# Keys with queries, and v, in two tiles; their loads issued in the middle of a step of the recurrence

## The chip, the cores and the metric

The kernel runs on one core of a Trainium2 chip. A core has TensorE (PE in the rows; its weight loads are PEld), VectorE (DVE), ScalarE (ACT), GpSimd (POOL) and SyncE (SP), which issues most transfers. The metric is the time of one execution on the device in microseconds, as the median of several.

## The reference, cut to what matters

Three stages follow each other. The change lies in the first.

```python
# q, k, v, f_logit: [B=4, H=8, S=768, D=48], f32
f = 1.0 / (1.0 + np.exp(-f_logit))
for t in range(S):                       # gated linear attention
    state = f[:, :, t, :, None] * state + np.einsum('bhd,bhe->bhde', k[:, :, t], v[:, :, t])
    y[:, :, t] = np.einsum('bhd,bhde->bhe', q[:, :, t], state)
x = y as [3072, 384]
# soft mixture of 8 experts: softmax of x @ phi over tokens, two weight products an expert, softmax back
# then gate * val @ w_out, with gate = sigmoid(x @ w_gate), val = x @ w_val
```

## The kernel before, in words

The recurrence is cut into 24 steps: 6 chunks of T = 128 positions (u) times 4 batches (b), step i = 4u + b. A step handles all 8 heads of one batch and one chunk. The order on each engine is the order in which the code is written; a pool only adds the waits that its tiles need. Work is written ahead, so that step i also prepares steps i + 1 to i + 5.

What stands in step i, in this order:

- POOL: `prep_k(i+1)` (line 326, two instructions: the keys times decays e, in place in the tile of keys), `z_stage(i+1)` (lines 335 and 337: the state times a decay, into sb), `prep_c(i+3)` (line 298: a clamp on the gate logits f).
- ACT: `conv_a(i+1)` in steps 1, 4, 7, 10, 13 and 16 alone (line 425: reads a raw piece of a gate weight), `prep_a(i+3)` (lines 302 and 303, on f), `prep_e(i+2)` (lines 316 and 317: decays e and rx from the sums s), copies of x and of transposed keys (lines 162 and 153), `y_out(i)` (line 403: empties y).
- PE: `a_stage(i)` (line 349, queries with keys), `y_inter(i)` (line 385, the products with the state sb), `prep_s(i+2)` (line 310, sums s of f), `kv(i)` (line 367), transposes (lines 159 and 152), in every fourth step `l_stage` (line 169) and in the one after it the products of lines 202 to 221, and at the end `y_intra(i)` (line 397, the masked products with v).
- DVE: `m_stage(i)` (line 356), `prep_q(i+1)` (line 330, queries times rx), z and the conversion of raw weights.
- SP: `load_f(i+5)`, in six steps a raw piece (`load_raw`, 512 KB), one load of expert weights (768 KB), and last `load_kq(i+3)`.

Keys, queries and v of one step lie in one tile `kqv` of 128 x 1408 numbers (704 KB), filled by one transfer; there are three such tiles, taken in turn (i % 3). So `load_kq(i+3)` overwrites what step i reads, and SP holds it until the last reader is done: `y_intra(i)`, which reads v. SP issues in order, and a transfer that waits holds up those behind it.

y and s each have one PSUM tile: `y_inter(i+1)` waits until `y_out(i)` has emptied y, and `prep_s(i+2)` until line 317 has read s.

Of the kernel before, what the change touches and what calls it, by code (L numbers as in the profile page):

```python
# [17 lines left out]
B, H, S, D = 4, 8, 768, 48  # L18
DM = H * D
TH = 64  # L20
HP = H // 2
T = 128
NU = S // T
# [6 lines left out]
NG = DFF // GW  # L30
QF = NF // NG
CONV_AT = 2, 5, 8, 11, 14, 17
KQ = 2 * HP * T
LOAD_FROM, LOAD_TO = 1, NSTEP - 1
WARM = 10, 1, 0, 0, 3, 1
BIG = 3.4e38
# [3 lines left out]
HUGE = float(np.uint32((1150 << 20) | 0xFFFFF).view(np.float32))  # L40


def body(ctx, tc, fn, fd, kqv, phi, w1, w2, wg, wv, wo, out_t):
    nc = tc.nc
    V, A, PE, PO, SP = nc.vector, nc.scalar, nc.tensor, nc.gpsimd, nc.sync

# [82 lines left out]
    def attention_in(att, aps, slow):  # L129
        def at(shape, tag, dt=F32):  # L130
            return att.tile(shape, dt, tag=tag, name=tag)
# [17 lines left out]
        def kt_stage(k, kts):  # L149
            ps = pt([128, HP, 112], "m", 2, "ktp")  # L150
            for h in range(HP):
                PE.transpose(ps[:, h], k[0:112, h], ident[0:112, 0:112])
            A.copy(kts, ps)
# [60 lines left out]
        def d2b(u):  # L214
            d2b_mm(u)
            d2b_add(u)
# [22 lines left out]
        def fast_steps():  # L239

            kq, vts, ft = [None] * 3, [None] * 3, [None] * 3

            def inputs(i):
                t = at([128, KQ + DM], f"kqv{i}")
                kq[i] = t[:, 0:KQ].rearrange("p (k h t) -> p k h t", k=2, t=T)
                vts[i] = t[:, KQ:].rearrange("p (j c) -> p j c", j=2)
                kqvs[i] = t

            kqvs = [None] * 3
            rrs = [at([128, 2, 2, T], f"r{j}") for j in range(2)]  # L250
            mask = at([128, 2, T], "mask")
            inputs(2)
# [38 lines left out]

            def load_kq(i):
                u, b = divmod(i, B)
                SP.dma_start(kqvs[i % 3], kqv[u, b])


            def prep_c(i):
                PO.tensor_scalar(ft[i % 3], ft[i % 3], FMIN, None, op0=ALU.max)  # L298
# [147 lines left out]
            def once(fn, i, *a):  # L446
                if 0 <= i < NSTEP:
                    fn(i, *a)
# [5 lines left out]
            load_f(1)  # L454
            load_f(2)
            load_kq(1)
            prep_c(0)
            make_tri()
            prep_c(1)
# [26 lines left out]
            for i in range(NSTEP):  # L486
                u, b = divmod(i, B)
                more = u < NU - 1
                cv = conv(i)

                if i:
                    once(prep_k, i + 1, PO)
                    once(z_stage, i + 1, PO)
                once(prep_c, i + 3)
                conv_a(i + 1)

                a_stage(i)
                for j in range(2):
                    m_stage(j)
                if i >= B:  # L500
                    y_inter(i)
                if i == 0:
                    kt_stage(kq[0][:, 0], kts)

                once(prep_a, i + 3)
                once(prep_s, i + 2)
                once(load_f, i + 5)
                load_raw(CONV_AT.index(i + 2) if i and i + 2 in CONV_AT else NP if i == CONV_AT[-1] + 1 else -1)
                load_weights(i, 0)
                once(prep_e, i + 2)  # L510
                if i:
                    once(prep_q, i + 1, V)

                cv[0]()
                cv[1]()
                if more:
                    kv(i)
                    z_add(i)

                if i:  # L520
                    x_stage(i - 1)
                if i + 1 < NSTEP - B:
                    kt_stage(kq[(i + 1) % 3][:, 0], kts)
                if i >= 4 and b == 0:
                    l_stage(u - 1)
                    d1(u - 1)
                if i >= 4 and b == 1:
                    d2(u - 1)
                    d1b(u - 1)
                cv[2]()  # L530
                cv[3]()
                y_intra(i)
                y_out(i)
                if i >= 4 and b == 1:
                    d2b(u - 1)
                if i >= 4 and b == 0:
                    d1e(u - 1)
                once(load_kq, i + 3)
                if i == NSTEP - 3:
                    constants()  # L540

        def slow_steps():
            wt = [at([128, HP, T], f"w{i}") for i in range(2)]
            kk = at([128, HP, T], "k")
            vts = [at([128, 2, HP * D], f"v{i}") for i in range(2)]
            qq = at([128, HP, 2, T], "q")
            kts = at([128, HP, 112], "kt")
            zps = [pt([128, 2, HP, D], f"z{i}") for i in range(2)]
            aps_ = [pt([128, 2, 2, T], f"a{i}") for i in range(2)]

            def slow_step(i):
                u, b = divmod(i, B)
                w = wt[1][0:112]
                for j in range(2):
                    d = slice(64 * j, 64 * j + D)
                    SP.dma_start(wt[1][d], fd[u, b, j])
                    SP.dma_start(kk[d], kqv[u, b, d, 0:HP * T])
                    SP.dma_start(qq[d, :, j], kqv[u, b, d, HP * T:KQ].rearrange("d (h t) -> d h t", t=T))
                SP.dma_start(vts[i % 2], kqv[u, b, :, KQ:].rearrange("t (j c) -> t j c", j=2))
                A.activation(w, w, AF.Exp, scale=-1.0)  # L560
                V.tensor_scalar(w, w, 1.0, None, op0=ALU.add)
                V.reciprocal(w, w)
                kt_stage(kk, kts)
                vv, s, q = vts[i % 2], sb[i % 2], qq
                vo, vm = [t.rearrange("p j (h e) -> p h j e", e=D) for t in (vv, vts[(i + 1) % 2])]
                z = zps[b % 2][:, b // 2]
                with tc.For_i(0, T, 1) as t:
                    V.tensor_tensor(
                        z[0:112], z[0:112], w[:, :, bass.ds(t, 1)].to_broadcast([112, HP, D]), op=ALU.mult
                    )  # L570
                    for h in range(HP):
                        V.tensor_tensor(
                            vm[:, h], vo[:, h], (ident, wt[0].rearrange("p h t -> p (h t)"))[h % 2][:, None, bass.ds(t, 1)].to_broadcast([128, 2, D]),
                            op=ALU.mult,
                        )
                    for h in range(HP):
                        for j in range(2):
                            PE.matmul(
                                z[64 * j:64 * j + D, h], kts[:, h, 64 * j:64 * j + D],
                                vts[(i + 1) % 2][:, j, h * D:h * D + D],  # L580
                                start=False, stop=True, skip_group_check=True,
                            )
                    V.tensor_copy(s[0:112], z[0:112])
                    for h in range(HP):
                        PE.matmul(
                            aps_[h // 2][0:D, h % 2, :, bass.ds(t, 1)], s[0:112, h], q[0:112, h, :, bass.ds(t, 1)],
                            start=True, stop=True, skip_group_check=True,
                        )
                for h in range(2):
                    for g in range(2):  # L590
                        A.copy(yts[i % 4][64 * h:64 * h + D, 2 * g:2 * g + 2], aps_[g][0:D, h])

            V.memset(wt[1][32:64], 30.0)
            V.memset(kk[32:64], 0.0)
            for t in zps + aps_:
                V.memset(t, 0.0)
            load_phi(SP)
            constants()
            for t in [qq] + yts:
                PO.memset(t, 0.0)  # L600
            for p in range(E * 2):
                load_w1(*divmod(p, 2))
            for e in range(3):
                load_w2(e, slice(0, 8))
            load_wo(0, 11)
            r = wt[0].rearrange("p h t -> p (h t)")
            V.tensor_copy(r[:, 0:TH], ident[:, TH:T])
            V.tensor_copy(r[:, TH:T], ident[:, 0:TH])
            for i in range(NSTEP):
                u = i // B  # L610
                slow_step(i)
                if i == NSTEP - 1:
                    break
                x_stage(i)
                if i % B == B - 1:
                    l_stage(u)
                    d1(u)
                    d1e(u)
                    d2(u)
                    d1b(u)  # L620
                    d2b(u)
# [5 lines left out]
        mb, u = mrun[(NU - 1) % 2], NU - 1  # L627
# [414 lines left out]
```

## Time and profile before

| | us |
|---|---|
| median of 3 executions | 403.28 (403.27 to 405.97) |
| the profiled execution | 405.25 |
| its span, first to last instruction | 403.5 |
| PE busy | 354.2 (88%) |
| DVE busy | 224.5 |
| ACT busy | 212.2 |
| POOL busy | 193.3 |

1.75 us of the profiled execution lie outside its span. The 24 steps of the recurrence end at about 165 us of the span; the experts and the gated product fill the rest. The mean granted clock of PE is 0.977 of full speed. The busy shares are means over stages with different limits; what the change touches is read from the stretch of the 24 steps.

### The profile page before, as it was taken

The page shows a single profiled execution, that of the slowest core. Times are in us where ns is not written, and L with a number is a line of the kernel's source. Part 1 is how long each engine was busy: PE and PEld are TensorE (multiplying, and loading weights), DVE is VectorE, ACT ScalarE, POOL GpSimd, SP SyncE. Part 2 cuts the span into 40 slices and gives each one's busy share as a digit, 9 for nine tenths or more (in the row PEclk, how much of TensorE's full clock was granted, in tenths as well). Part 3 has the DMA queues.
Part 4 walks back from the last instruction along what each step waited for, and adds up shares of the span by engine and source line. Part 5 has one row for each costly group of instructions (what it writes and reads, how often), then busy time and mean ns, then how long its engine had stood idle before and what let it go on. Part 6 is the DMA issues. An engine that isn't in the chain of part 4 may idle for free.

```text
span 403.5 us, 9261 instructions
## 1 busy us (share of the span) xinstructions
PE 354.2 (88%) x3790; PEld 275.0 (68%) x3790; DVE 224.5 (56%) x419; ACT 212.2 (53%) x437; POOL 193.3 (48%) x210
## 2 busy tenths in 40 slices
PE   2877996969877958999788999999999999999993
PEld 2766775757666846734456887688888787888882
DVE  2763654562635534468628776536777667444442
ACT  4556572746466534323456766566555465544440
POOL 5265537355365433002116666465565556655550
PEclk9998998998999998999989999999999999999999
DMA  6667896795878895599500421040000000222222
GB/s 227 233 211 280 272 325 234 261 345 206 282 277 313 305 410 226 218 373 411 251 0 0 158 80 79 0 156 2 0 0 2 0 2 1 78 80 78 78 81 87
DMA packets 15588, 66.81 MB, mean 166 GB/s; under 512 B 1728, under 2 KB 5168, under 8 KB 14000
## 3 DMA queue, kind: packets, MB, share of 16 engines
q1 hardware_dynamic: 15408, 66.07, 44.5%
q8 instruction: 32, 0.52, 0.5%
q14 instruction: 20, 0.16, 0.1%
q10 hardware_dynamic: 128, 0.06, 0.0%
HBM read 61.40 MB, written 4.72 MB: 164 GB/s over the span
## 4 chain that ended last, share of the span: by engine, by line


## 5 line engine op out<-in xcount | busy, mean ns | idle before, releaser
L890 POOL TENSOR_TENSOR hl<-sg,hh 128x512 fp32r<-128x512 f32 x72 | 99.7, 1385 | 84.7 <-ACT hh L888 75.4
L886 DVE TENSOR_TENSOR sg<-sg,gvp 128x512 f32<-128x512 f32 x72 | 49.5, 687 | 68.6 <-ACT sg L885 68.2
L918 PE MATMUL oup<-hh,wo 128*128 128x512 f32 x216 | 84.8, 392 | 1.5 <-ACT acc L900 1.3
L919 PE MATMUL oup<-hh,wo 128*128 128x512 f32 x216 | 84.1, 389 | 0.0
L888 ACT CAST hh<-sg 128x512 fp32r<-128x512 f32 x72 | 44.8, 622 | 55.8 <-DVE sg L886 55.8
L326 POOL TENSOR_TENSOR kqv<-kqv,e 112x256 f32<-112x256 f32 x44 | 33.9, 792 | 71.0 <-DMA kqv<-kqv 46.8
L885 ACT ACTIVATE sg<-gvp 128x512 f32<-128x512 f32 x72 | 42.9, 596 | 17.3 <-PE gvp L880 16.9
L918 PEld LDWEIGHTS oup<-hh,wo 128*128 128x128 f32 x216 | 40.5, 188 | 12.0 <-ACT acc L900 1.7
L356 DVE TENSOR_TENSOR r<-a,mask 128x512 f32<-128x512 f32 x48 | 30.9, 685 | 29.7 <-PE a L349 29.6
L919 PEld LDWEIGHTS oup<-hh,wo 128*128 128x128 f32 x216 | 40.5, 188 | 8.2
L925 PE MATMUL oup<-hl,wo 128*128 128x512 f32 x162 | 45.6, 390 | 0.0
L880 PE MATMUL gvp<-cs,gs 128*128 128x512 f32 x144 | 44.7, 392 | 0.4 <-DVE sg L886 0.2
L310 PE MATMUL s<-tri,f 128*48 128x128 f32 x384 | 30.3, 308 | 9.6 <-ACT f L303 6.2
L302 ACT ACTIVATE f<-f 128x384 f32<-128x384 f32 x24 | 12.5, 522 | 45.3 <-POOL f L298 45.3
L925 PEld LDWEIGHTS oup<-hl,wo 128*128 128x128 f32 x162 | 30.3, 188 | 6.5 <-POOL hl L890 0.2
L310 PEld LDWEIGHTS s<-tri,f 128*48 128x48 f32 x384 | 23.2, 138 | 14.5 <-POOL tri L272 6.0
L298 POOL TENSOR_SCALAR f<-f 128x384 f32<-128x384 f32 x24 | 29.7, 1238 | 4.1 <-DMA f<-fn 4.0
L880 PEld LDWEIGHTS gvp<-cs,gs 128*128 128x128 f32 x144 | 26.9, 188 | 6.9 <-ACT gs L871 0.7
L706 POOL TENSOR_TENSOR wo<-wf,wo 128x384 fp32r<-128x384 f32 x12 | 12.2, 1016 | 38.7 <-PE hp L748 25.9
L385 PE MATMUL y<-kqv,sb 48*48 48x128 f32 x320 | 13.9, 289 | 16.3 <-ACT yt L403 10.0
L397 PE MATMUL y<-r,kqv 128*48 128x128 f32 x384 | 26.8, 283 | 0.4 <-DVE r L356 0.4
L397 PEld LDWEIGHTS y<-r,kqv 128*48 128x48 f32 x384 | 20.4, 126 | 4.8 <-issue 1.8
(153 smaller groups left out, 563.6 us busy)
## 6 DMA issues: line engine op xcount, KB each, us to landing
kqv<-kqv SPq DMA_DIRECT2D x24, 704.0 KB, 5.9
w<-w SPq DMA_DIRECT2D x22, 768.0 KB, 6.3
f<-fn SPq DMA_DIRECT2D x24, 192.0 KB, 3.5
rawo<-wo SPq DMA_DIRECT2D x3, 1536.0 KB, 7.5
w2p<-w SPq DMA_DIRECT2D x3, 1536.0 KB, 10.6
out_t<-os SPq DMA_DIRECT2D x17, 256.0 KB, 2.1
w<-w SPq DMA_DIRECT2D x2, 1536.0 KB, 8.1
rawg<-wg SPq DMA_DIRECT2D x2, 1536.0 KB, 7.5
```

The lines of the kernel that those rows point to most:

```text
L310: PE.matmul(sps[64 * j:64 * j + D, h], w[:, h, j], tri, start=True, stop=True, skip_group_check=True,)
L326: eng.tensor_tensor(k[:, h], k[:, h], e[:, h, :, ::1 - 2 * h], op=ALU.mult)
L356: V.tensor_tensor(rrs[j].rearrange("p g h t -> p g (h t)"), aps_[:, j].rearrange("p g h t -> p g (h t)"), mask.rearrange("p h t -> p (h t) ...
L397: PE.matmul(yps[64 * h:64 * h + D, j, g], vv[:, j, c:c + D], rrs[j][:, g, h], start=(i < B and g == 0), stop=True, skip_group_check=True,)
L880: PE.matmul(p, gs[n, k][:, o:o + 128], cs[:, u].rearrange("p b t -> p (b t)"), start=True, stop=True)
L885: A.activation(sg, ps[0], AF.Sigmoid)
L886: V.tensor_tensor(sg, sg, ps[1], op=ALU.mult)
L888: A.copy(h, sg)
L890: PO.tensor_tensor(l, sg, h.bitcast(F32), op=ALU.subtract)
L918: PE.matmul(ops[u][c], wh[q][:, fq, cc[c]], h, start=(fq == 0), stop=False)
L919: PE.matmul(ops[u][c], wl[q][:, fq, cc[c]], h, start=False, stop=False)
L925: PE.matmul(ops[u][c], wh[q][:, fq, cc[c]], l, start=False, stop=False)
```

## The change

Keys and queries lie in a tile `kq` of 128 x 1024 (512 KB), v in a tile of 128 x 384 (192 KB). Each has three buffers. Their loads stand right behind `y_inter(i)` in the code, ahead of `load_f(i+5)`: `load_kq(i+3)` and `load_v(i+2)`. At the start, v of steps 0 and 1 is loaded behind the keys of step 1. On the host the array `kqv` is given as two arrays. No instruction of another engine is added, dropped or moved. (Line numbers behind the edits differ by some lines.)

```diff
-def body(ctx, tc, fn, fd, kqv, phi, w1, w2, wg, wv, wo, out_t):
+def body(ctx, tc, fn, fd, kqd, v, phi, w1, w2, wg, wv, wo, out_t):
...
             def inputs(i):
-                t = at([128, KQ + DM], f"kqv{i}")
-                kq[i] = t[:, 0:KQ].rearrange("p (k h t) -> p k h t", k=2, t=T)
-                vts[i] = t[:, KQ:].rearrange("p (j c) -> p j c", j=2)
-                kqvs[i] = t
-
-            kqvs = [None] * 3
+                kq[i] = at([128, 2, HP, T], f"kq{i}")
+                vts[i] = at([128, 2, HP * D], f"v{i}")
+
...
             def load_kq(i):
                 u, b = divmod(i, B)
-                SP.dma_start(kqvs[i % 3], kqv[u, b])
+                SP.dma_start(kq[i % 3].rearrange("p k h t -> p (k h t)"), kqd[u, b].rearrange("p k c -> p (k c)"))
+
+            def load_v(i):
+                u, b = divmod(i, B)
+                SP.dma_start(vts[i % 3], v[b, u * T:(u + 1) * T].rearrange("t (j c) -> t j c", j=2))
...
             load_f(1)
             load_f(2)
             load_kq(1)
+            load_v(0)
+            load_v(1)
             prep_c(0)
...
                     y_inter(i)
                 if i == 0:
                     kt_stage(kq[0][:, 0], kts)
+                once(load_kq, i + 3)
+                once(load_v, i + 2)
 
                 once(prep_a, i + 3)
                 once(prep_s, i + 2)
...
                     d1e(u - 1)
-                once(load_kq, i + 3)
                 if i == NSTEP - 3:
                     constants()
```

On SP, steps 5 to 7 before (step 6 has a raw piece). A row is a transfer with its tile, its source and its shape; kqv is the joint tile, f the gate logits, w expert weights, raw a piece of the gate weights:

```order
L290 DMA f_130<-fn 128x384
L96 DMA w_1_523<-w 128x1536
L294 DMA kqv_116<-kqv 128x1408
L290 DMA f_129<-fn 128x384
L418 DMA raw<-wg 128x1024
L96 DMA w_2_720<-w 128x1536
L294 DMA kqv_126<-kqv 128x1408
L290 DMA f_131<-fn 128x384
L96 DMA w_2_720<-w 128x1536
L294 DMA kqv_121<-kqv 128x1408
```

and the same steps now (kq of steps 8, 9 and 10, v of steps 7, 8 and 9):

```order
L290 DMA kq_116<-kq 128x1024
L294 DMA v_123<-v 128x384
L286 DMA f_133<-fn 128x384
L95 DMA w_1_534<-w 128x1536
L290 DMA kq_128<-kq 128x1024
L294 DMA v_117<-v 128x384
L286 DMA f_132<-fn 128x384
L418 DMA raw<-wg 128x1024
L95 DMA w_2_733<-w 128x1536
L290 DMA kq_122<-kq 128x1024
L294 DMA v_129<-v 128x384
L286 DMA f_134<-fn 128x384
```

The load of step i + 3's keys has moved from behind the step's weights to ahead of its f, and what it waits for is `y_inter(i)`; v has a row of its own, one step nearer to its use, and waits for `y_intra(i-1)`, which is past by then.

The start of SP before:

```order
L290 DMA f_129<-fn 128x384
L294 DMA kqv_121<-kqv 128x1408
L290 DMA f_131<-fn 128x384
L290 DMA f_130<-fn 128x384
L418 DMA raw<-wg 128x1024
L294 DMA kqv_116<-kqv 128x1408
L290 DMA f_129<-fn 128x384
L294 DMA kqv_126<-kqv 128x1408
```

and now:

```order
L286 DMA f_132<-fn 128x384
L290 DMA kq_122<-kq 128x1024
L294 DMA v_129<-v 128x384
L294 DMA v_123<-v 128x384
L286 DMA f_134<-fn 128x384
L286 DMA f_133<-fn 128x384
L418 DMA raw<-wg 128x1024
L290 DMA kq_116<-kq 128x1024
L290 DMA kq_128<-kq 128x1024
L294 DMA v_117<-v 128x384
L286 DMA f_132<-fn 128x384
```

The keys of step 2 keep their place behind the raw piece; those of step 3 now follow them at once, ahead of the f of step 5.

## Rows read from the trace of the kernel before

**Rows 1.** Windows from one a_stage to another, then two shorter ones; columns in the first line.

```profile
core 0: us, PE busy (x) PEld busy (x) DVE busy (x) ACT busy (x) POOL busy (x), PEclk, DMA share, GB/s
16.50:43.05 26.55, 20.35 (x402) 17.15 (x401) 13.11 (x23) 14.94 (x34) 16.15 (x23) 0.94 0.75 260
43.05:70.96 27.91, 22.68 (x461) 18.70 (x459) 15.81 (x29) 15.25 (x37) 14.20 (x21) 0.94 0.77 267
70.96:98.15 27.19, 22.77 (x460) 18.70 (x459) 13.51 (x26) 15.60 (x38) 14.06 (x20) 0.94 0.76 266
98.15:124.57 26.42, 21.16 (x461) 17.45 (x459) 12.75 (x25) 15.74 (x39) 11.34 (x18) 1.00 0.86 300
124.57:147.39 22.82, 19.91 (x437) 16.19 (x435) 12.34 (x24) 11.54 (x29) 11.29 (x16) 1.00 0.88 329
147.39:164.70 17.31, 12.82 (x235) 9.57 (x236) 7.10 (x15) 7.58 (x23) 6.13 (x12) 0.90 0.56 221
164.70:403.50 238.80, 225.67 (x1232) 169.88 (x1229) 142.32 (x261) 122.43 (x221) 112.56 (x85) 0.99 0.24 94
67.40:70.70 3.30, 3.30 (x46) 2.80 (x48) 1.30 (x5) 0.34 (x1) 2.13 (x4) 0.50 0.06 18
138.00:148.00 10.00, 8.21 (x193) 6.81 (x193) 4.01 (x9) 2.93 (x7) 4.43 (x7) 1.00 1.01 417
```

**Rows 2.** Waits from 20 to 164 us: us in total, times, longest.

```profile
POOL kqv L326 <- DMA kqv<-kqv: 46.8, 10, 7.1
ACT f L302 <- POOL f L298: 41.1, 15, 6.2
...
PE y L385 <- ACT yt L403: 10.0, 5, 4.1
...
PE l L169 <- ACT x L162: 5.7, 4, 3.7
```

**Rows 3.** Timeline of steps 10 to 12: start, us, instruction, idle before it and its releaser.

```profile
79.64 0.60 ACT L316 ACTIVATE e<-s 112x512 f32<-112x512 f32 x1 [0.26 <-PE s L310]
...
82.66 0.65 PE L385 MATMUL y<-kqv,sb 48*48 48x128 f32 x16
...
83.38 2.18 POOL L326 TENSOR_TENSOR kqv<-kqv,e 112x256 f32<-112x256 f32 x2 [5.10 <-DMA kqv<-kqv]
...
84.79 0.33 SPq L290 DMA_DIRECT2D f<-fn  x1
...
86.33 1.60 POOL L298 TENSOR_SCALAR f<-f 128x384 f32<-128x384 f32 x1
...
87.22 0.33 SPq L294 DMA_DIRECT2D kqv<-kqv  x1
87.96 0.52 ACT L302 ACTIVATE f<-f 128x384 f32<-128x384 f32 x1 [5.45 <-POOL f L298]
...
90.73 0.63 ACT L403 COPY yt<-y 112x512 f32<-112x512 f32 x1
...
91.50 1.11 PE L385 MATMUL y<-kqv,sb 48*48 48x128 f32 x16 [3.54 <-POOL gg L335]
```

**Rows 4.** Transfers by kind: count, KB each, median us from issue to landing.

```profile
kqv<-kqv SPq DMA_DIRECT2D x24, 704.0 KB, 5.9
...
f<-fn SPq DMA_DIRECT2D x24, 192.0 KB, 3.5
...
raw<-wg SPq DMA_DIRECT2D x3, 512.0 KB, 4.2
```

**Rows 5.** Timeline of ACT in step 7.

```profile
56.35 0.69 ACT L425 ACTIVATE wgv<-raw 128x512 f32<-128x512 f32 x1 [1.75 <-DMA raw<-wg]
```

**Rows 6.** Timeline of PE, the a_stage of steps 7 and 8.

```profile
53.90 0.90 PE L349 MATMUL a<-kqv 48*64 48x128 f32 x32
...
58.63 0.90 PE L349 MATMUL a<-kqv 48*64 48x128 f32 x32
```

**Rows 7.** Timeline of POOL, the prep_k of steps 2 and 3.

```profile
24.13 1.33 POOL L326 TENSOR_TENSOR kqv<-kqv,e 112x256 f32<-112x256 f32 x2 [1.68 <-ACT e L316]
...
29.21 1.33 POOL L326 TENSOR_TENSOR kqv<-kqv,e 112x256 f32<-112x256 f32 x2 [1.68 <-ACT e L316]
```

More of the change, by code (lines that the diff above doesn't have):

```diff
@@ L32 @@
 CONV_AT = 2, 5, 8, 11, 14, 17
-KQ = 2 * HP * T
 LOAD_FROM, LOAD_TO = 1, NSTEP - 1
@@ L556, in slow_step @@
                     SP.dma_start(wt[1][d], fd[u, b, j])
-                    SP.dma_start(kk[d], kqv[u, b, d, 0:HP * T])
-                    SP.dma_start(qq[d, :, j], kqv[u, b, d, HP * T:KQ].rearrange("d (h t) -> d h t", t=T))
-                SP.dma_start(vts[i % 2], kqv[u, b, :, KQ:].rearrange("t (j c) -> t j c", j=2))
+                    SP.dma_start(kk[d], kqd[u, b, d, 0])
+                    SP.dma_start(qq[d, :, j], kqd[u, b, d, 1].rearrange("d (h t) -> d h t", t=T))
+                SP.dma_start(vts[i % 2], v[b, u * T:(u + 1) * T].rearrange("t (j c) -> t j c", j=2))
                 A.activation(w, w, AF.Exp, scale=-1.0)
@@ L1009 @@
         "f": np.ascontiguousarray(heads_t(f_logit)),
-        "kqv": np.concatenate([
-            np.pad(
-                np.stack([kr.reshape(NU, B, 2, D, HP * T), heads_t(q)], axis=4),
-                ((0, 0), (0, 0), (0, 0), (0, 64 - D), (0, 0), (0, 0)),
-            ).reshape(NU, B, 128, KQ),
-            vr.reshape(B, NU, T, DM).transpose(1, 0, 2, 3),
-        ], axis=3),
+        "kq": np.pad(
+            np.stack([kr.reshape(NU, B, 2, D, HP * T), heads_t(q)], axis=4),
+            ((0, 0), (0, 0), (0, 0), (0, 64 - D), (0, 0), (0, 0)),
+        ).reshape(NU, B, 128, 2, HP * T),
+        "v": np.ascontiguousarray(vr.reshape(B, S, DM)),
         "phi": np.pad(
```

## The prediction, made before the changed kernel ran

> **What bounds the kernel now.** I read the windows first, cut at an a_stage every fourth step, so that five stretches B to F follow the first one, A [rows 1]. Behind 164.70 us PE works 225.67 of 238.80 us: that part is set by its own products, and the change has no instruction in it. Of the 24 steps, A loses 6.2 us of PE time (26.55 - 20.35), and B to F lose 5.23, 4.42, 5.26, 2.91 and 4.49, together 22.3. PE also works part of the time at half clock: in 67.40 to 70.70 it was granted 0.50 of full speed, which is the lower of its two levels (1.2 GHz), after it had idled in front of the product of line 169. The cost is the stretch times one minus the granted share: 27.91 x 0.06, 27.19 x 0.06 and 17.31 x 0.10, so 1.7, 1.6 and 1.7 in B, C and F, together 5.0. So 27.3 us are lost in B to F, and no engine is full there: POOL, DVE and ACT each work about half of the time.
>
> What ends these waits is seen in the table of waits [rows 2]. PE waits for y to be emptied (10.0 us) and for copies of x (5.7). ACT, which empties y and copies x, waits 41.1 us for POOL's clamp on f. And POOL waits 46.8 us in ten waits for the transfer of kqv, up to 7.1 us. The timeline shows how one of these becomes PE's wait [rows 3]. Step 11's prep_k starts at 83.38, 5.10 us after POOL's last work, released by the transfer. The decay e that it also needs was done at 79.64 + 0.60 = 80.24, so 3.1 us of it are the transfer's alone. The clamp stands behind prep_k on POOL and runs at 86.33, ACT starts on f at 87.96 after 5.45 us idle, and everything behind that on ACT is late: y of step 11 is emptied at 90.73 to 91.36. POOL's next state comes in the same moment, and y_inter of step 12 starts at 91.50, 3.54 us late. That is one chain, transfer, POOL, ACT, PE, and it closes on itself, since SP issues the next kqv only when PE is through with y_intra.
>
> **The change, part by part.** The load of the keys is held by y_inter in place of y_intra. In step 11 y_inter ends at 82.66 + 0.65 = 83.31 and the load went out at 87.22: 3.9 us earlier now, more in steps where PE waits between the two. It also carries 512 KB in place of 704 and stands ahead of f and the step's weights on SP. A transfer of 704 KB landed after 5.9 us, one of 512 KB (raw) after 4.2, in the median [rows 4]; so the keys should be there some 1.7 us sooner still, 5.6 us in all. The transfer's own share of the wait was 3.1 us in step 11. I therefore take these waits as gone, and what is late next on POOL is e, which comes from ACT.
>
> What comes back must be taken off the 27.3 us. First, without a late transfer POOL and ACT feed each other in a round of their own: prep_k, clamp, ACT's work on f and e, next prep_k. In steps 2 and 3, where POOL waited for e and for no transfer, it took 29.21 - 24.13 = 5.08 us [rows 7]. A short step of PE takes 58.63 - 53.90 = 4.73 [rows 6]. Two of four steps are that short (the others have line 169, or lines 202 to 221, on top), so each of B to E keeps 2 x 0.35, together 2.8 us. Below that it can't go unless POOL works faster; if the long steps give the lag back it is nothing.
>
> Second, the raw pieces. ACT reads one in five steps, ahead of its work on f, and in step 7 it stood 1.75 us for it [rows 5]. Its load is held by prep_s through the f in front of it, so it goes out no earlier than now, and what stood ahead of it as kqv of the step before, issued at that step's end, is now kq and v of this step, issued just ahead. It can land earlier, if the steadier flow keeps the queue short, or later by up to the difference of the medians of 704 KB and 192 KB, 5.9 - 3.5 = 2.4 us. The transfer that it most resembles is itself, so I take 1.75 us as the wait in each of B to E, 7.0 in all; the bounds are 0 and 4 x (1.75 + 2.4) = 16.6. Third, the copies of x that line 169 waits for are ACT's, and ACT stays busier in that step than in others: a quarter of the 5.7 us, 1.4, stays (bounds 0 and 5.7).
>
> Edits at nothing: the 24 further issues of v cost SP 0.33 us each (the time of the issue in rows 3), 7.9 us in all, but SP mostly waits; what they push back are f, used two steps later, weights, used after the recurrence, and raw, counted above. v lands a step before kv reads it; if it did not, PE would stand in line 367. In stretch A, the keys of step 2 keep their place behind f and raw; the stretch is paced by the round of 5.08 us [rows 7], which nothing shortens, so I take 0; the bounds are 0 and the 1.7 us by which a smaller transfer landed sooner.
>
> Sum: 27.3 - 2.8 - 7.0 - 1.4 = 16.1 us less. The end moves with the recurrence, since PE is full behind it. The profiled execution of 405.25 would become 389.2; it stood 1.97 above the median, 403.28, which becomes 387.2.
>
> **Rivals.**
>
> *The transfer queues are full.* The 16 engines are busy 0.77, 0.76, 0.86 and 0.88 of B to E [rows 1], so 21.5 + 20.7 + 22.7 + 20.1 = 85.0 of 104.3 us. The forecast takes about 10 us out of these four (F gives the rest), which leaves 94: 90% busy. In D, 22.7 us of transfers would stand in some 24. Then keys would wait behind the weights of the step before, and POOL would wait for transfers as now, less often. For it speaks that the rate in B and C is 267 GB/s at 0.77, so no more than 350 at full; against it, that 138 to 148 moved 417 GB/s, in long rows of weights. Half of the waits gone would be 8 us less: 395. The Trainium skill (DMA: Bandwidth & Descriptors, Specifications) gives about 358 GB/s as the limit of HBM for a core; by it the 30.1 MB of B to E (27.91 x 267 + 27.19 x 266 + 26.42 x 300 + 22.82 x 329) would take an estimated 84 us, the same floor as the busy sum, and the end could not come below about 383. The 417 GB/s of that window speak against it as a limit.
>
> *Raw becomes the bound: slower.* Kq and v go out ahead of raw in the same burst. ACT reads raw ahead of f, so a late piece holds up decays, copies and the emptying of y in five steps. Without the raw term the sum is 23.1 us; raw would have to hold ACT 23.1 / 5 = 4.6 us a time for nothing to be left. At 6 us, which is 704 KB in the queue ahead of it (5.9 us), with nothing else ahead, the five cost 30 and the kernel takes 403.3 + 30 - 23.1 = 410. Against it: in step 11 the f, which stands ahead of raw, went out at 84.79, 1.5 us after the end of y_inter at 83.31 [rows 3], so the first 1.5 us of those 5.9 are past when raw goes out.
>
> *Hidden behind the recurrence, or not earlier at all.* The load is held by y_inter, and y_inter is what comes late; or the expert weights, which keep the pace of the steps, are not there when the recurrence ends sooner. F has its transfers busy for 0.56 of 17.31 us, so 7.6 us of room stand against the second, and step 11 against the first. If only the half-clock cost and F's idle were won back, 5.0 + 4.5 less the terms that stay there, it would be about 4 us less than now: 399.
>
> **How the numbers follow.** One per cent is 4.0 us, about what a measurement of this kernel can tell from no change. Forecast: 0.70. Full queues: 0.18. Raw as the bound: 0.06. Little won: 0.06. The range's lower end takes raw and the round at half their terms: 27.3 - 1.4 - 3.5 - 1.4 = 21.0, and 1.7 of stretch A, 22.7 less: 380. The upper end is full queues with raw late as well, a third of the forecast's gain, 5 less: 398. Faster by over 1%: 0.70, 0.15 of the full queues, 0.02 of the last, 0.87. Within 1%: 0.03 + 0.04 and a little of raw, 0.08. Slower: 0.05.
>
> **What would show it.** Right: in the table of waits, POOL for the transfer of kq falls from 46.8 us to under 10, POOL for e takes its place, and ACT's wait for the clamp halves. The stretches B to E last 23 to 25 us each (E 20 to 21) and have one half-clock piece at most; the transfer share is about 0.9. Raw's step: ACT's waits for raw in line 425 add up to about 7 us; if they reach 20, the second rival is right. Full queues: transfer share over 0.95, kq landing later than 6 us in the median. The forecast is wrong if y_inter still waits over 8 us in all while POOL no longer waits for kq: then ACT's own order would have been the bound.

## The result and the profile after

| | before | changed |
|---|---|---|
| median of 4 executions each, us | 404.58 (403.27 to 405.97) | 393.5 (391.84 to 394.98) |
| profiled execution, us | 405.25 | 393.43 |
| its span, us | 403.5 | 391.7 |

The ratio is 0.9725, 95% interval 0.9665 to 0.9784: faster by 2.75%, 11 us. The forecast was 387.2 with a range of 380 to 398. That forecast started from a median of 403.28, to which a fourth execution has been added since. The sign and the range hold; of the 16.1 us forecast, 11 to 12 came.

The windows of the changed kernel, cut at the same a_stage rows as [rows 1], A to F and the rest:

```profile
core 0: us, PE busy (x) PEld busy (x) DVE busy (x) ACT busy (x) POOL busy (x), PEclk, DMA share, GB/s
16.81:41.32 24.51, 19.92 (x402) 17.26 (x401) 13.06 (x23) 14.87 (x34) 16.53 (x23) 0.93 0.82 289
41.32:68.95 27.63, 22.60 (x461) 18.54 (x459) 15.13 (x29) 15.23 (x37) 14.47 (x20) 0.94 0.81 274
68.95:92.77 23.82, 21.10 (x461) 17.60 (x459) 13.38 (x26) 15.33 (x38) 12.96 (x20) 0.99 0.84 286
92.77:120.72 27.95, 22.70 (x461) 18.36 (x459) 12.88 (x25) 15.97 (x39) 13.19 (x21) 0.94 0.85 302
120.72:140.92 20.20, 19.86 (x437) 16.19 (x435) 12.93 (x24) 14.08 (x35) 10.53 (x16) 1.00 0.79 289
140.92:152.99 12.07, 11.40 (x235) 8.43 (x236) 7.70 (x15) 5.14 (x16) 4.36 (x8) 1.00 0.98 400
152.99:391.70 238.71, 225.57 (x1232) 169.91 (x1230) 142.39 (x261) 122.43 (x221) 112.61 (x85) 0.99 0.24 94
```

Beside [rows 1] the first column of each row, its length, changes like this. The last line splits the forecast by stretch: PE's loss and its half-clock cost, less what the prediction left of the round, of raw and of the copies.

| stretch | A | B | C | D | E | F | rest |
|---|---|---|---|---|---|---|---|
| before, us | 26.55 | 27.91 | 27.19 | 26.42 | 22.82 | 17.31 | 238.80 |
| after, us | 24.51 | 27.63 | 23.82 | 27.95 | 20.20 | 12.07 | 238.71 |
| difference | -2.0 | -0.3 | -3.4 | +1.5 | -2.6 | -5.2 | -0.1 |
| forecast | 0 | -4.1 | -3.2 | -2.5 | -0.1 | -6.2 | 0 |

With 0.3 us at the start these add up to the 11.8 us between the spans. The total looks like a forecast that is a third too large; by stretch it is something else. C came as forecast, F 1.0 short of it, A and E gave 2.0 and 2.5 more, and B and D together gave nothing where 6.6 us were expected. The gain is missing in two places, and the waits point at why.

The waits of the changed kernel from 20 to 153 us (us in total, times, longest):

```profile
POOL kq L326 <- ACT e L316: 49.1, 17, 5.1
...
ACT f L302 <- POOL f L298: 19.7, 12, 2.7
...
PE l L168 <- ACT x L161: 6.4, 4, 3.0
POOL kq L326 <- DMA kq<-kq: 6.4, 2, 5.2
ACT wgv L425 <- DMA raw<-wv: 6.3, 3, 3.0
...
PE y L385 <- ACT yt L403: 5.8, 3, 2.9
...
ACT wgv L425 <- DMA raw<-wg: 3.7, 1, 3.7
```

Against [rows 2] the first chain is gone: POOL's wait for keys fell from 46.8 us in ten waits to 6.4 in two, and ACT's wait for the clamp from 41.1 to 19.7. POOL now waits 49.1 us for the decays e, which come from ACT. Line 425, ACT's reading of a raw piece, waits 10.0 us in four waits (6.3 + 3.7). Before, its waits were 1.75 [rows 5], 0.54 and 1.50, so 3.8.

The timeline of steps 6 to 8 in B shows what hangs on one of them (start, us, instruction, idle before it and its releaser):

```profile
50.57 0.43 SPq L418 DMA_DIRECT2D raw<-wg  x1
...
52.58 1.16 POOL L298 TENSOR_SCALAR f<-f 128x384 f32<-128x384 f32 x1
...
56.61 0.67 ACT L425 ACTIVATE wgv<-raw 128x512 f32<-128x512 f32 x1 [3.74 <-DMA raw<-wg]
...
57.19 0.51 ACT L302 ACTIVATE f<-f 128x384 f32<-128x384 f32 x1
...
58.16 0.58 ACT L316 ACTIVATE e<-s 112x512 f32<-112x512 f32 x1
...
58.82 2.15 POOL L326 TENSOR_TENSOR kq<-kq,e 112x256 f32<-112x256 f32 x2 [5.08 <-ACT e L316]
...
59.95 0.63 ACT L403 COPY yt<-y 112x512 f32<-112x512 f32 x1
...
60.72 0.66 PE L385 MATMUL y<-kq,sb 48*48 48x128 f32 x16 [2.92 <-ACT yt L403]
...
65.47 0.82 PE L168 MATMUL l<-yt,phs 112*32 112x128 f32 x16 [1.81 <-ACT x L161]
```

It is the chain of [rows 3] with another head. The clamp on f was done at 53.74, so ACT could have gone on with f by then. It stands in line 425 until 56.61 for a piece that went out at 50.57, and f, e, prep_k, the emptying of y and y_inter follow late one after the other. PE loses 2.92 us here, 1.81 more in line 168, and has a half-clock piece behind it: in 65.40 to 68.90 it was granted 0.56 of full speed, and B as a whole 0.94, as before. By stretch, line 425 waits 3.74 us in B, 2.12 in C and 1.24 + 2.99 in D. B and D, with the most, are the two stretches without a gain; C gained in spite of its wait.

Did the piece come later, or did ACT come sooner? The same piece before, its issue and that of the transfer ahead of f, with its use in [rows 5] at 56.35:

```profile
48.70 0.33 SPq L294 DMA_DIRECT2D kqv<-kqv  x1
51.76 0.33 SPq L290 DMA_DIRECT2D f<-fn  x1
52.13 0.43 SPq L418 DMA_DIRECT2D raw<-wg  x1
```

and the last two transfers ahead of it now:

```profile
49.04 0.33 SPq L290 DMA_DIRECT2D kq<-kq  x1
49.41 0.64 SPq L294 DMA_DIRECT2D v<-v  x1
```

ACT was free for the piece 2.5 us after its issue before (56.35 - 1.75 - 52.13) and 2.3 us after it now (56.61 - 3.74 - 50.57), so it did not come sooner. The piece came later: it was used 4.2 us after its issue before, and 6.0 now. The joint transfer used to go out 3.4 us ahead of it; the keys now go out 1.5 us ahead. While the piece was under way, the 16 engines were busy for 0.88 of the time before (52.13 to 56.35), and now for 0.92 and then 1.01 (50.57 to 52.87 to 56.61). The pieces of steps 10, 13 and 16 show the same: used 3.8, 4.4 and 4.5 us after their issue before (the second without a wait), 5.1, 6.7 and 6.0 now.

Transfers by kind (count, KB each, median us from issue to landing), beside [rows 4]:

```profile
w<-w SPq DMA_DIRECT2D x22, 768.0 KB, 7.3
kq<-kq SPq DMA_DIRECT2D x24, 512.0 KB, 4.1
f<-fn SPq DMA_DIRECT2D x24, 192.0 KB, 4.0
v<-v SPq DMA_DIRECT2D x24, 192.0 KB, 4.8
...
raw<-wg SPq DMA_DIRECT2D x3, 512.0 KB, 4.9
raw<-wv SPq DMA_DIRECT2D x3, 512.0 KB, 6.0
```

Keys land after 4.1 us in place of 5.9. What now stands behind them lands later: f after 4.0 in place of 3.5, raw of wg after 4.9 in place of 4.2, raw of wv after 6.0 in place of 4.4.

### The profile page after: what moved, and what is told of

Read it like the earlier page. It is cut to its first block, busy times and chain, and to the rows that moved or that the text cites. A ratio compares the mean times of both kernels' runs of the same rounds, so it can differ in the third digit from the quotient of the medians.

```text
span 391.7 us, 9305 instructions
## 1 busy us (share of the span) xinstructions
PE 352.9 (90%) x3790; PEld 274.5 (70%) x3790; DVE 225.1 (57%) x419; ACT 212.5 (54%) x437; POOL 192.4 (49%) x210
## 4 chain that ended last, share of the span: by engine, by line
## 5 line engine op out<-in xcount | busy, mean ns | idle before, releaser
L326 POOL TENSOR_TENSOR kq<-kq,e 112x256 f32<-112x256 f32 x44 | 32.9, 768 | 63.5 <-ACT e L316 49.1
L888 ACT ACTIVATE sg<-gvp 128x512 f32<-128x512 f32 x72 | 42.9, 596 | 17.2 <-PE gvp L883 16.9
L310 PE MATMUL s<-tri,f 128*48 128x128 f32 x384 | 29.2, 300 | 8.9 <-ACT f L303 5.8
L397 PE MATMUL y<-r,v 128*48 128x128 f32 x384 | 27.0, 284 | 0.7 <-DVE r L356 0.7
L349 PEld LDWEIGHTS a<-kq 48*64 48x64 f32 x768 | 19.3, 141 | 7.5 <-issue 6.4
L397 PEld LDWEIGHTS y<-r,v 128*48 128x48 f32 x384 | 20.4, 126 | 5.0 <-issue 1.8
```

The lines of the kernel that those rows point to most:

```text
L310: PE.matmul(sps[64 * j:64 * j + D, h], w[:, h, j], tri, start=True, stop=True, skip_group_check=True,)
L326: eng.tensor_tensor(k[:, h], k[:, h], e[:, h, :, ::1 - 2 * h], op=ALU.mult)
L397: PE.matmul(yps[64 * h:64 * h + D, j, g], vv[:, j, c:c + D], rrs[j][:, g, h], start=(i < B and g == 0), stop=True, skip_group_check=True,)
L888: A.activation(sg, ps[0], AF.Sigmoid)
```

## The experiments

My theory after the result: the move of the keys does what the prediction says, and the raw pieces, which the same move pushes back in SP's burst, take a good part of it away again. The rivals: the queues are full (then raw or keys wait whatever their order), the split alone or the smaller transfer does it, or v's place matters. All times are compared by the ratio to the kernel before on the same chip, since its median differs by chip: 404.58 us beside the changed kernel, 406.72 beside x1 to x4, 406.2 beside x6 to x10, 404.44 beside x11 and x13. Each trace is of one execution.

| kernel | median us | ratio, 95% interval |
|---|---|---|
| changed kernel | 393.5 | 0.9725 [0.9665, 0.9784] |
| x1: changed, raw a step earlier | 382.06 | 0.9408 [0.9331, 0.9486] |
| x2: changed, raw behind the weights | 409.25 | 1.0082 [1.0039, 1.0125] |
| x3: before, raw a step earlier | 407.36 | 1.0019 [0.9961, 1.0077] |
| x4: split alone, loads at the end of a step | 403.55 | 0.9917 [0.9873, 0.9961] |
| x6: changed, kq and v behind f and raw | 393.47 | 0.9683 [0.9623, 0.9743] |
| x8: changed, v at the end of a step | 393.36 | 0.9652 [0.9582, 0.9722] |
| x9: x4 with raw a step earlier | 402.28 | 0.9872 [0.982, 0.9924] |
| x10: x1, last weight piece two steps later | 381.34 | 0.9358 [0.9306, 0.9411] |
| x11: x6, last weight piece two steps later | 386.19 | 0.9522 [0.9427, 0.9616] |
| x13: changed, last weight piece two steps later | 393.56 | 0.9734 [0.9668, 0.98] |

**Raw a step earlier (x1_raw_early).** Each raw piece goes out one step earlier than in the changed kernel; the queue carries the same bytes.

```diff
-                load_raw(CONV_AT.index(i + 2) if i and i + 2 in CONV_AT else NP if i == CONV_AT[-1] + 1 else -1)
+                load_raw(CONV_AT.index(i + 3) if i + 3 in CONV_AT else NP if i == CONV_AT[-1] + 1 else -1)
```

> The changed kernel with each raw piece loaded one step earlier (its tile has three slots, so nothing new has to be waited for). Theory raw: ACT's wait for raw (10.0 us in four waits in the changed kernel) is what keeps B and D as long as before, so it goes to under 2 us and the time to 384 to 388. Theory full queues: the bytes are the same, only earlier, so the lateness moves to kq or f and the time stays at 391 to 394. Theory round: the round of POOL and ACT of 5.1 to 5.7 us is what is left, so raw's wait goes but the time falls by under 2 us.

Its windows of A to F and the rest, with the columns of the windows above:

```profile
18.29:40.43 22.14, 19.81 (x403) 17.39 (x401) 12.35 (x23) 14.98 (x34) 15.25 (x23) 0.92 0.82 290
40.43:64.11 23.68, 21.55 (x460) 17.56 (x458) 14.62 (x29) 15.50 (x37) 13.71 (x20) 1.00 0.89 314
64.11:87.09 22.98, 21.10 (x460) 17.53 (x459) 13.83 (x25) 15.57 (x38) 13.02 (x20) 1.00 0.91 328
87.09:110.06 22.97, 21.10 (x460) 17.44 (x458) 13.05 (x25) 15.94 (x39) 13.32 (x21) 1.00 0.88 318
110.06:131.07 21.01, 20.16 (x436) 16.22 (x434) 12.97 (x24) 14.12 (x35) 10.56 (x16) 1.00 0.89 333
131.07:143.70 12.63, 11.54 (x235) 8.40 (x236) 6.79 (x15) 5.15 (x16) 3.85 (x8) 1.00 0.87 356
143.70:380.90 237.20, 224.25 (x1232) 169.32 (x1232) 142.47 (x261) 122.71 (x221) 112.83 (x85) 1.00 0.24 94
```

and its waits from 20 to 144 us:

```profile
POOL kq L326 <- ACT e L316: 42.0, 18, 4.4
...
ACT f L302 <- POOL f L298: 15.8, 14, 2.2
...
PE y L385 <- ACT yt L403: 2.9, 2, 2.3
...
PE l L168 <- ACT x L161: 2.4, 3, 1.3
...
PE dtp L201 <- ACT x L161: 1.4, 4, 0.5
```

Line 425 has no wait left, B and D are 4.0 and 5.0 us shorter than in the changed kernel, and B to E run at full clock. The median is below the 384 to 388 expected. By the ratios the kernel is faster than the changed one by 3.2% of the time of before, some 13 us, give or take 4 (the two intervals taken together); by the spans of the profiled executions it is 391.7 - 380.9 = 10.8. Of these, 9.0 lie in B to E, where the waits for raw were: PE idles 6.6 us less there and works 2.4 less, at full clock. So the 10.0 us of raw's waits cost about as much as they last; that they cost more is not shown. The rest of the 13 us is not located.

The full queues as the bound of the step fall here: with a share of 0.88 to 0.91 and the keys landing after a median of 5.1 us, later than in the changed kernel, nothing on POOL waits for them between 20 and 130 us. The same bytes fill the queue even more, and where each transfer has a step of slack this costs nothing here.

**Raw later (x2_raw_late).** The opposite step: raw stands behind the step's weights.

```diff
-                load_raw(...)
                 load_weights(i, 0)
+                load_raw(...)
```

> The changed kernel with raw issued behind the step's expert weights (768 KB more ahead of it). Theory raw: it lands some 2 us later, ACT's wait for it grows from 10.0 to 17 to 20 us, and the time goes to 398 to 402. Theory round: ACT has slack, so within 1.5 us of 393.5. Theory full queues: the same bytes in the same step, within 1.5 us of 393.5.

Two rows of its timeline, ACT at the raw piece of step 16 and PE behind it:

```profile
123.87 0.66 ACT L425 ACTIVATE wgv<-raw 128x512 f32<-128x512 f32 x1 [5.68 <-DMA raw<-wv]
...
126.95 1.30 PE L168 MATMUL l<-yt,phs 112*32 112x128 f32 x20 [5.68 <-ACT x L161]
```

The waits of line 425 add up to 19.6 us in five, inside the 17 to 20 expected, but the time is not: 409.25, 0.8% slower than before, where 398 to 402 were expected. By the ratios it is 3.6% behind the changed kernel (0.0357 x 404.58 = 14 us). The trace is of the fastest of its ten executions, 404.29, with a span of 402.6, so it shows 10.9 us of that: there ACT waits 9.6 us more for raw. ACT's delay reaches PE in full in line 168 above. In B to E, 9.45 us longer than in the changed kernel (109.05 in place of 99.60), PE idles 5.7 us more and works 3.7 longer, at a granted 0.92 in place of 0.97. The prediction's second rival, raw as the bound, is thus real in its mechanism: with raw one place further back in the queue the changed kernel is slower than before, by 0.8%, interval 0.4 to 1.3.

**The same step without the change (x3_before_raw_early).** The edit of x1 in the kernel before.

> The kernel before with raw one step earlier. Theory raw: there the transfer of kqv bounds, and raw's wait was 3.8 us in three waits, so 0 to 3 us less than before: 401 to 404.5. If raw had bounded before as much as now, 396 or less.

No difference (1.0019). POOL still waits for the joint transfer:

```profile
POOL kqv L326 <- DMA kqv<-kqv: 45.3, 10, 6.9
```

Raw's wait is worth nothing that can be told from noise while the keys come late, and 3.2% once they come in time. The two edits don't add: 1.0019 and 0.9725 alone, 0.9408 together. That is why the small wait seen before was no measure of its price afterwards.

**The split without the move (x4_split_only).** Two tiles, both loads at the end of a step.

```diff
             load_kq(2)
+            load_v(2)
...
-                once(load_kq, i + 3)
-                once(load_v, i + 2)
...
                     d1e(u - 1)
+                once(load_kq, i + 3)
+                once(load_v, i + 3)
```

> The two tiles, but both loads at the end of the step, where the joint one stood (v of step i+3 behind kq of step i+3). If the gain is the earlier issue: kq lands sooner only by its smaller size, at most 1.7 us of each of ten waits, and half of that reaches the end, so 396 to 402. If the smaller transfer is what matters: 394 or less. The reader of v still holds v's load, so f and raw of the next step wait behind it as before.

0.8% faster. Its transfers of keys and its wait for them (20 to 164 us):

```profile
kq<-kq SPq DMA_DIRECT2D x24, 512.0 KB, 7.1
```

```profile
POOL kq L326 <- DMA kq<-kq: 25.2, 6, 7.1
```

A transfer of 512 KB behind the step's weights lands after 7.1 us, later than the 704 KB of before (5.9) and than the 512 KB of the changed kernel (4.1), which go out ahead of them. It is also issued sooner than before. The keys no longer wait for y_intra, so they follow the issue of the weights by a median of 0.53 us, where the joint transfer followed by 2.21. Counted from the weights, the keys land after some 7.6 us (0.53 + 7.1) and landed after some 8.1 (2.21 + 5.9). So the earlier issue that the split alone allows is nearly used up behind the weights, and in the middle of the recurrence 192 KB less bring little. Of the 3.4 us gained (0.0083 x 404.58) about a third is at the start: step 5's a_stage starts at 41.93 here, against 43.05 before and 41.32 in the changed kernel. With raw a step earlier on top, the two tiles still give no more than 1.3%:

> Two tiles, both loads at the end of a step, and raw one step earlier: all of the faster version but the earlier issue of kq. If the earlier issue is what the gain needs: POOL still waits 25 to 45 us for kq, 398 to 404. If raw alone held ACT: 390 or less.

x9 comes out at 0.9872, against 0.9408 for x1. So the place ahead of the weights is needed; neither the split nor raw stands in for it.

**Keys behind raw (x6_kq_behind_raw).** Here kq and v go out ahead of the weights, but behind f and raw.

```diff
-                once(load_kq, i + 3)
-                once(load_v, i + 2)
...
                 load_raw(...)
+                once(load_kq, i + 3)
+                once(load_v, i + 2)
                 load_weights(i, 0)
```

> The changed kernel with kq and v issued behind f and raw, still ahead of the expert weights: the same burst in another order. Theory raw: 704 KB less stand ahead of raw, so it lands some 1.5 to 2 us sooner, ACT's wait for it falls from 10.0 us to 3 to 5, and the time to 386 to 390; kq lands by the same later and POOL still doesn't wait for it. Theory full queues: POOL waits for kq again (over 20 us) and the time is 393 or more.

Missed: 0.9683, not told apart from the changed kernel. Raw's waits fell to 6.0 us (3.5 + 2.5), but POOL waited 12.0 us for keys, 3.05 and 3.39 behind raw pieces and 5.60 at the end of the recurrence. Its windows, B to E as one and then F:

```profile
39.81:133.08 93.27, 83.51 (x1810) 68.67 (x1808) 53.73 (x103) 58.55 (x143) 50.08 (x76) 1.00 0.88 317
133.08:150.90 17.82, 14.19 (x235) 10.60 (x236) 7.10 (x15) 7.57 (x22) 5.25 (x9) 0.81 0.64 261
```

B to E are 6.3 us shorter than in the changed kernel (99.60), as theory raw expects, and F gives 5.8 of it back (17.82 against 12.07). The same `load_raw` sends, in step 18, the first piece of the output weights (`rawo`, 1.5 MB), which now stood ahead of the keys. SP's queue, then POOL:

```profile
121.58 0.38 SPq L108 DMA_DIRECT2D rawo<-wo  x1
122.05 0.38 SPq L290 DMA_DIRECT2D kq<-kq  x1
...
130.47 1.83 POOL L326 TENSOR_TENSOR kq<-kq,e 112x256 f32<-112x256 f32 x2 [5.60 <-DMA kq<-kq]
```

Keys that went out at 122.05 are used at 130.47, after 5.60 us of POOL's idling. To test that reading, x11 is x6 with `rawo` two steps later, behind kq and v:

```diff
+                load_raw(CONV_AT.index(i + 2) if i and i + 2 in CONV_AT else -1)
                 once(load_kq, i + 3)
                 once(load_v, i + 2)
+                load_raw(NP if i == NSTEP - 4 else -1)
```

> Kq and v behind f and raw as in the run before, but the 1.5 MB piece of the last weight, which shares raw's call and so had come to stand ahead of the keys of step 21, two steps later and behind them. Theory raw: the 3.19 us wait of y_inter at 137 us of that run and the half-clock stretch behind it go, so 386 to 389. If the order of raw and kq in the burst gains nothing by itself: 392 to 394.

As expected, 386.19 and 0.9522. The same two windows show where it comes from, since B to E stay and F falls back to the length that it has in the changed kernel:

```profile
40.75:134.65 93.90, 85.50 (x1810) 70.03 (x1808) 54.84 (x103) 60.99 (x149) 51.50 (x78) 0.98 0.88 310
134.65:146.42 11.77, 11.32 (x235) 8.43 (x236) 6.55 (x15) 5.15 (x16) 2.78 (x7) 1.00 1.02 411
```

Two more apply the later `rawo` where it stands behind the keys anyway, to see that it is worth nothing by itself: in the changed kernel (x13) and in x1 (x10).

```diff
-... NP if i == CONV_AT[-1] + 1 else -1)
+... NP if i == NSTEP - 4 else -1)
```

> The changed kernel with that piece of the last weight two steps later and nothing else. PE had no wait over 0.7 us behind 125 us in the changed kernel, so theory raw expects no gain: 393.5 within 1.5 us. If the end of the recurrence was held by that piece there too: 391 or less.

> Raw one step earlier, and the 1.5 MB piece of the last weight, which stood ahead of the keys of steps 22 and 23, issued two steps later. POOL's wait for kq (8.3 us, in two waits at the end of the recurrence) goes to under 2 us. Since PE had only 0.64 us of waits there, 381 to 382.5: as with raw early alone. If the end of the recurrence was held by it, 379.

x13 is at 0.9734, the changed kernel at 0.9725. x10 is at 0.9358, and its interval overlaps that of x1. x1 and x10 are the fastest kernels here, and are not told apart. (Of the 8.3 us of x1 that x10's expectation puts at the end of the recurrence, 4.46 lie at the start, before step 2's prep_k at 17.82.)

**The place of v (x8_v_at_end).** kq stays in the middle of a step, v goes out at its end, for step i + 3.

```diff
             load_kq(2)
+            load_v(2)
...
-                once(load_v, i + 2)
...
+                once(load_v, i + 3)
```

> The changed kernel with kq in the middle of a step, and v of step i+3 at its end, where it is held by the last reader of v, and f and raw of the next step stand behind it. If v's place ahead of raw costs: raw lands some 0.5 us sooner, 391 to 393. If it is only that keys come early: 393.5 within 1.5 us.

0.9652, overlapping with the changed kernel. Raw's waits stay at 10.5 us (5.8 + 4.7). So the 192 KB of v are not what delays raw; of what the change put ahead of it that leaves the keys, and x6, which sends both behind raw, does cut the waits.

## Why the prediction was right, and where its size was off

- *The chain, transfer, POOL, clamp, ACT, PE.* Right. POOL's wait for keys fell to 6.4 us (under 10 was the sign), ACT's wait for the clamp halved, e took the transfer's place, PE idles 6.9 us in all before y_inter, 5.8 of it for ACT (under 8).
- *The load goes out earlier, 3.9 us, and ahead of f and the weights.* Right as the cause, though the two are not separated in full: x4 and x9, where the keys also go out sooner but behind the weights, gain 0.8 and 1.3%.
- *A smaller transfer lands 1.7 us sooner.* The 1.8 us came (4.1 after 5.9), but not by the size: the same 512 KB took 7.1 us behind the weights (x4), so the place ahead of them did it. At the start, where the prediction took 0, some came: step 2's prep_k, at 19.37 before, is at 17.69, and at 17.0 to 18.6 in all traces with two tiles, and A is 2.0 us shorter, just past its bound of 1.7.
- *What is lost, 27.3, less the round and the copies: 23.1 without the raw term.* The total of x1, where that term is gone, is close to it, 403.5 - 380.9 = 22.6 us less span, but that is in part luck. B to F are only 18.4 us shorter; A with the start gives 2.6 (43.05 - 40.43), and the part behind the recurrence 1.6, which no step foresaw. There PE was granted 1.00 in place of 0.99; in x10 the same part was granted 0.97 and took 240.10 us, so it varies from one execution to the next.
- *The round, 2.8, and the copies, 1.4.* **The copies were sized too small.** In B to E x1 keeps 6.7 us of PE idle where both were put at 4.2. PE's waits for copies of x come to 3.8 (2.4 in line 168 and 1.4 in line 201, of which the prediction counted the first alone); of the rest, 0.6 is y_inter's wait for ACT, and for 2.3 the trace names no releaser. So the round came out smaller than its 2.8, or can't be told from that remainder.
- *Raw, 7.0 us.* **The wait was sized too small as well.** The prediction had the mechanism (kq and v ahead of raw in the same burst, ACT reading raw ahead of f), and then took the wait of before, 1.75, since "the transfer that it most resembles is itself". Its landing did not stay: the four pieces were used 1.3 to 2.3 us later after their issue than before, inside the 2.4 that it had as a bound, and the waits came to 10.0 us in all. Taking them away shortened B to E by 9.0 (by 5.9 between x13 and x10, 96.09 and 90.23, where x13's trace is of its fastest execution), and the kernel by 11 to 13. The bounds, 0 to 16.6, held.
- *The sum by stretch.* In B to F, 6.1 of the 16.1 us are missing. Raw accounts for some 2.0 of them (9.0 against 7.0), what x1 still lacks in B to E for 3.2 (9.9 + 7.0 = 16.9 expected without raw, 104.34 - 90.64 = 13.7 came), F for 1.0. That the whole fell only 4.3 us short, 11.8 of 16.1, is because A and the start gave 1.7 unforeseen. Each of these is from one execution a kernel.
- *Raw, one piece in each of B to E.* Wrong: the steps that read it are 4, 7, 10, 13 and 16, so D has two (1.24 and 2.99) and E none. That fits D losing 1.5 us and E winning 2.6, and with raw early D is 5.0 us shorter (x1).
- *B to E at 23 to 25 us, one half-clock piece at most, a share of 0.9.* Right for C and E, wrong for B and D of the changed kernel (27.6, 23.8, 28.0 and 20.2; pieces in B and D; 0.79 to 0.85), right for all in x1 (23.7, 23.0, 23.0, 21.0; no piece; 0.88 to 0.91). The forecast described the kernel without raw's wait.
- *Full queues, the rival of 0.18.* The time came near its 395, but its signs did not: no share over 0.95 in B to E, and kq landing after 4.1 us. The queue was full in a smaller sense, for the few us in which raw stood in it (a share of 1.01 in 52.87 to 56.61), and one step more of lead ended that wait with a higher share over the stretch (x1). In F, where the share is 0.98, POOL did wait 6.4 us for keys, and PE idled for 0.7 us in all.
- *Nothing lost behind the recurrence.* Right: 238.71 against 238.80.

What stays open: the medians put raw at 13 us and the traces at 9.0 in B to E and 10.8 in all, and no run shows where the difference lies. How much of the keys' gain is the earlier issue and how much the place ahead of the weights was not separated either.

## What to carry to other kernels

A load that is moved forward moves those behind it back. List the burst in order of issue with the slack of each reader, and move the load with the least slack forward along with it: here one more step of lead for the raw pieces, which the kernel before didn't need, doubled the gain. Price a transfer by what stands ahead of it in the queue, not by its own bytes alone. And the wait seen at a load while something else bounds the step is no measure of its price once that is gone: here 3.8 us, worth nothing, became 10.0, worth 3.2%.

## What the runs showed of the hardware

The same 512 KB landed after a median of 4.1 us ahead of the step's weights (changed kernel) and 7.1 us behind them (x4). In F of the changed kernel the transfers moved 400 GB/s over 12.07 us at a share of 0.98, and before 417 GB/s over 10 us [rows 1]. The Trainium skill gives about 358 GB/s as the limit for a core (DMA: Bandwidth & Descriptors, Specifications). As a cap that doesn't hold in these traces of a kernel on one core, and the floor that a rival of the prediction rested on it isn't shown by them. B to E took 90.2 us or more in every run, above that floor's 84.
